# Moving the pools of the large tiles to the front of SBUF, behind a 384-byte pad, in a decode forward-and-backward kernel

## Chip, cores and metric

One core of one Trainium2 chip. The metric is the device time of one execution in microseconds (us), lower is better. A ratio is the mean time of one kernel's fast runs over the mean of the other's fast runs of the same rounds, so it is not quite the ratio of the medians that are quoted beside it. A difference under 2% is called "same"; the intervals are 95% intervals.

## The reference

Two attention layers on a long key and value cache and two small MLPs, for a batch of 2 and one token each, and then all gradients. Cut to what matters:

```python
B, Sq, D = 2, 1, 1024
Hq, Hkv, Sk, Dh = 32, 4, 16384, 128        # k_cache, v_cache: (2, 4, 16384, 128) bf16
# wq (1024, 4096), wo (4096, 1024); w1 (1024, 3584), w2 (3584, 1024)
x = x + attention(layernorm(x), k_cache, v_cache, wq, wo)
x = x + mlp(layernorm(x), w1, b1, w2, b2)
x = x + attention(layernorm(x), ...)       # the same weights and cache again
x = x + mlp(layernorm(x), ...)
# returned: x, and the gradients of x, k_cache, v_cache, wq, wo, w1, b1, w2, b2
```

The arithmetic per byte is tiny. The caches (33.6 MB each) are read several times, their gradients are written once.

## The kernel before

Transfers are nearly all of 1 MB: 128 partitions, 4096 bf16 values (8192 bytes) in each. Loads go out on the sync engine's queue, stores on GpSimd's. Seven rotating load tiles and ten kept tiles take all of them.

```python
LDW, NLD = 4096, 7
const = ctx.enter_context(tc.tile_pool(name="const", bufs=1))   # identities, masks
vec = ctx.enter_context(tc.tile_pool(name="vec", bufs=1))       # small vectors
pers = ctx.enter_context(tc.tile_pool(name="pers", bufs=1))     # e_all, 32768 bytes a partition
ld = ctx.enter_context(tc.tile_pool(name="ld", bufs=NLD))       # 7 load tiles of 8192 bytes
res = ctx.enter_context(tc.tile_pool(name="res", bufs=1))       # 10 kept tiles of 8192 bytes
ktp = ctx.enter_context(tc.tile_pool(name="ktp", bufs=4))       # and further pools
# ... cut ...
def w_load(W, j0, rb, n_cols):               # a chunk of a weight: rb rows of n_cols in a partition
    wt = ld.tile([128, LDW], BF16, name="wt", tag="ld")
    wv = wt[:, 0:rb * n_cols].rearrange("p (j n) -> p j n", j=rb)
    nc.sync.dma_start(wv, W[j0 * 128:(j0 + rb) * 128, :].rearrange("(j p) n -> p j n", p=128))
    return wv
# ... cut ...
def kv_load(w, g, c):                        # a chunk of a cache: one row of 8192 bytes in a partition
    keep = w + str(c) if g == G - 1 else w if (g, c) == (XG, 0) else None
    t = held_tiles[keep] if keep else ld.tile([128, LDW], BF16, name="kv_" + w, tag="ld")
    if keep not in held:
        src = Kv if w == "K" else Vv
        nc.sync.dma_start(t[:].rearrange("p (t d) -> p t d", d=128), src[g, :, c * TC:(c + 1) * TC, :])
        # ... cut ...
def store(out_ap, view, tile_):
    nc.gpsimd.dma_start(out_ap, view)
    by_store.append(tile_)                   # the tile is free for the next load
```

Until about 700 us there are nearly only loads (forward passes, and the backward parts that end in small vectors). From about 750 us on, the gradients of the caches and weights are made and stored while the caches are loaded once more, and load tiles and kept tiles serve both.

Tiles are laid out in the order of the pools, in steps of 32 bytes (the addresses here were read from the built programs, not from a trace). In the kernel before, the constants start at byte 16512 of the partition and e_all at 26048, which is 50 x 512 + 448. What follows it has sizes that are multiples of 512, so e_all, the seven load tiles and the ten kept tiles all begin 448 bytes past a multiple of 512, that is 192 past a multiple of 256.

## Time and profile before

| | before |
|---|---|
| median of 3 runs | 1155.29 us (1153.3 to 1155.74) |
| span of the profiled run, mean granted TensorE clock | 1151.1 us, 0.845 |
| moved by DMA | 449.30 MB, mean 390 GB/s |
| PE, DVE, ACT busy | 83%, 55%, 49% |

The page of the kernel before, the slices (40 of 28.8 us each; the first line has the busy share of the 16 DMA engines in tenths, the second what they moved) and the queues (q1 carries the loads, q0 the stores):

```profile
DMA  8999999998999999999999999888999999999996
GB/s 368 418 418 418 419 418 399 396 371 329 418 418 413 419 352 373 399 372 396 376 417 409 364 365 351 330 320 316 411 422 422 417 418 420 421 416 418 424 420 241
...
q1 hardware_dynamic: 72204, 348.17, 75.9%
q0 software_dynamic: 16752, 98.59, 20.7%
```

The engines for DMA are hardly ever idle, and there is a plateau of 418 GB/s in the slices with loads alone, and one of 418 to 424 in the last third, with stores beside the loads. The table by stretches says the same of chosen times. Its columns: from and to, length, then busy us and number of instructions of PE, weight loads, DVE, ACT and POOL, the granted clock, the DMA share and GB/s. The rows are two forward stretches (8192-byte rows), one with mostly rows of 2048 bytes (200 to 225 us), and two with stores.

```profile
50.00:150.00 100.00, 85.58 (x1625) 70.06 (x1622) 45.62 (x99) 42.45 (x190) 0.00 (x0) 0.85 1.01 418
300.00:400.00 100.00, 86.70 (x1709) 70.95 (x1701) 47.86 (x106) 44.53 (x201) 0.00 (x0) 0.90 1.01 417
200.00:225.00 25.00, 11.46 (x304) 10.44 (x304) 3.19 (x17) 0.00 (x0) 1.38 (x2) 0.50 1.01 396
...
850.00:950.00 100.00, 89.33 (x1146) 54.38 (x1146) 78.66 (x138) 72.12 (x139) 14.74 (x25) 0.80 1.01 420
1000.00:1100.00 100.00, 85.23 (x1165) 51.88 (x1165) 75.16 (x133) 70.31 (x136) 14.71 (x24) 0.85 1.02 420
```

A DMA share of 1.01 means that the packets' own times fill the stretch: there is no gap to close, and with the same bytes in the same rows only shorter packets can make it faster. The trace records every packet with its size and duration; a packet here is one row in one partition.

### The profile page before, as it was taken

What the parts mean: (1) busy time and instruction counts of PE and PEld (TensorE: products, weight loads), DVE (VectorE), ACT (ScalarE), POOL (GpSimd) and SP (SyncE); (2) the same over time, 40 slices, a digit from 0 to 9 for tenths busy, and PEclk for the clock granted to TensorE, in tenths of its full rate; (3) what the DMA queues carried; (4) which work ended last, traced back from release to release, by engine and by line L of the source; (5) the groups of instructions that cost most, each with busy time, mean ns of one, the idle gap of its engine ahead of it and who ended that gap; (6) DMA issues with size and microseconds to landing.
All of it is one profiled execution on the core that took longest, in us unless ns stands there. A gap on an engine that the chain in (4) does not pass through costs nothing. (4 is left out here: it accounts for less than half of the span.)

```text
span 1151.1 us, 39972 instructions
## 1 busy us (share of the span) xinstructions
PE 952.2 (83%) x17567; PEld 735.8 (64%) x17567; DVE 633.9 (55%) x1347; ACT 566.5 (49%) x1418; POOL 64.5 (6%) x117
## 2 busy tenths in 40 slices
PE   4989886487889875899998699988898998998786
PEld 3867674487767755898876588865555554555452
DVE  1545442132544441554746454678788866787684
ACT  0544351021544440344544344767677757687573
POOL 0000000000000000000000000001111111111111
PEclk9988886587997886899998899998888867799795
DMA  8999999998999999999999999888999999999996
GB/s 368 418 418 418 419 418 399 396 371 329 418 418 413 419 352 373 399 372 396 376 417 409 364 365 351 330 320 316 411 422 422 417 418 420 421 416 418 424 420 241
DMA packets 89130, 449.30 MB, mean 390 GB/s; under 512 B 7026, under 2 KB 7026, under 8 KB 49788
## 3 DMA queue, kind: packets, MB, share of 16 engines
q1 hardware_dynamic: 72204, 348.17, 75.9%
q0 software_dynamic: 16752, 98.59, 20.7%
q8 instruction: 137, 2.24, 0.8%
q14 instruction: 37, 0.30, 0.1%
HBM read 348.14 MB, written 98.58 MB: 388 GB/s over the span
## 5 line engine op out<-in xcount | busy, mean ns | idle before, releaser
L153 ACT COPY kT<-tp 128x512 int32<-128x512 int32 x209 | 122.6, 587 | 258.9 <-PE tp L419 248.2
L156 DVE COPY kT<-tp 128x1024 bf16<-128x1024 bf16 x159 | 108.7, 690 | 111.7 <-PE tp L419 99.8
L419 PE MATMUL tp<-ident,kv_K 128*128 128x128 bf16 x1728 | 145.6, 234 | 3.3 <-DMA kv_K<-in_A_k_cache_dram 3.3
L419 PEld LDWEIGHTS <-kv_K 128*128 128x128 bf16 x1728 | 110.7, 104 | 3.9 <-DMA kv_K<-in_A_k_cache_dram 3.8
L164 DVE CAST big<-xm 128x512 bf16<-128x512 f32 x135 | 88.1, 685 | 26.4 <-PE xm L1160 13.5
L161 ACT CAST big<-xm 128x512 bf16<-128x512 f32 x162 | 88.2, 593 | 27.0 <-PE xm L1160 15.7
L572 PEld LDWEIGHTS <-kT 128*128 128x128 bf16 x2048 | 76.8, 98 | 28.0 <-issue 22.2
L572 PE MATMUL sc<-qT_bf,kT 128*128 128x8 bf16 x2048 | 92.2, 171 | 0.5 <-issue 0.4
L269 PE MATMUL wtp<-ident,wt 128*128 128x128 bf16 x928 | 77.1, 231 | 3.8 <-issue 2.5
L419 PE MATMUL tp<-ident,kv_V 128*128 128x128 bf16 x864 | 71.0, 230 | 9.8 <-DMA kv_V<-in_A_v_cache_dram 9.0
L305 PEld LDWEIGHTS <-wt 128*128 128x128 bf16 x1696 | 48.9, 103 | 47.0 <-issue 15.4
L536 ACT ACTIVATE e_all<-sc,negm 128x64 bf16<-128x64 f32 x256 | 76.9, 344 | 1.1 <-DVE negm L531 1.0
L164 DVE CAST keepK<-xm 128x512 bf16<-128x512 f32 x91 | 59.0, 685 | 22.4 <-PE xm L1242 17.7
L451 PE MATMUL acc_all<-kv_V,e_all 128*16 128x256 bf16 x864 | 46.4, 294 | 29.0 <-DMA kv_V<-in_A_v_cache_dram 16.1
L156 DVE COPY wT<-wtp 128x1024 bf16<-128x1024 bf16 (+1 forms) x64 | 40.7, 641 | 50.8 <-PE wtp L269 47.3
L161 ACT CAST keepK<-xm 128x512 bf16<-128x512 f32 x105 | 56.8, 592 | 24.2 <-PE xm L1242 21.8
L153 ACT COPY wT<-wtp 128x512 int32<-128x512 int32 (+1 forms) x60 | 34.2, 571 | 66.2 <-PE wtp L269 57.5
L419 PEld LDWEIGHTS <-kv_V 128*128 128x128 bf16 x864 | 56.1, 103 | 11.7 <-DMA kv_V<-in_A_v_cache_dram 9.8
L269 PEld LDWEIGHTS <-wt 128*128 128x128 bf16 x928 | 58.8, 103 | 4.5 <-issue 3.1
L161 ACT CAST keepV<-xm 128x512 bf16<-128x512 f32 (+1 forms) x93 | 50.3, 594 | 21.6 <-PE xm L1242 16.8
L536 ACT ACTIVATION_READ_ACCUMULATOR e_all<-sc,negm 128x1 f32 x256 | 60.2, 236 | 0.0
L164 DVE CAST keepV<-xm 128x512 bf16<-128x512 f32 (+1 forms) x80 | 52.4, 685 | 12.7 <-PE xm L1242 9.1
(350 smaller groups left out, 1774.1 us busy)
## 6 DMA issues: line engine op xcount, KB each, us to landing
kv_K<-in_A_k_cache_dram SPq DMA_DIRECT2D x81, 1024.0 KB, 12.7
kv_V<-in_A_v_cache_dram SPq DMA_DIRECT2D x81, 1024.0 KB, 12.2
out_dram<-big POOLq DMA_DIRECT2D x36, 1024.0 KB, 21.0
wt<-in_A_wo_dram SPq DMA_DIRECT2D x32, 1024.0 KB, 10.6
wt<-in_B_w_dram SPq DMA_DIRECT2D x32, 896.0 KB, 14.6
out_dram<-keepK POOLq DMA_DIRECT2D x21, 1024.0 KB, 20.0
out_dram<-keepV POOLq DMA_DIRECT2D x19, 1024.0 KB, 18.6
wt<-in_A_wq_dram SPq DMA_DIRECT2D x16, 1024.0 KB, 9.2
```

The source lines that it names most:

```text
L153: S.copy(out=dst.bitcast(I32), in_=src.bitcast(I32))
L156: V.tensor_copy(out=dst, in_=src)
L161: S.copy(out=dst, in_=src)
L164: V.tensor_copy(out=dst, in_=src)
L269: PE.transpose(tp[:, o, :], wv[:, j, (o0 + o) * 128:(o0 + o + 1) * 128], ident[:])
L305: PE.matmul(fps[:, jo, :].rearrange("p (a b) -> p a b", b=2), lhsT=wv[:, j, jo * 128:(jo + 1) * 128], rhs=xT_bf[:, j0 + j, :].unsqueeze(1) ...
L419: PE.transpose(tp[:, j, :], cv[:, b * 8 + j, :], ident[:])
L451: PE.matmul(self.acc[cg:cg + 16, :], lhsT=coef(u), rhs=self.cv[:, t:t + 2, :].rearrange("p t d -> p (t d)"), start=False, stop=True, tile_ ...
L536: S.activation(out=e_all[:, g, f * half:(f + 1) * half, l, h, :], in_=sc[g][f][:, h, :].rearrange("p (a b) -> p a b", b=2), func=ACT.Exp, ...
L572: PE.matmul(sc[g][f][:, :, t % TH], lhsT=kT[:, j, :], rhs=q_bf[:, g, :], start=True, stop=True)
```

## The change

The intent: loads write into SBUF at starts that are a multiple of 512 bytes. The pools of the large tiles come first, behind a pad that fills up to the next multiple (16512 + 384 = 16896 = 33 x 512), and the pools with odd sizes come behind them. Nothing else is changed; both kernels have 39972 instructions and 89130 packets.

```diff
-    const = ctx.enter_context(tc.tile_pool(name="const", bufs=1))
-    vec = ctx.enter_context(tc.tile_pool(name="vec", bufs=1))
+    base = ctx.enter_context(tc.tile_pool(name="base", bufs=1))
+    base.tile([128, 192], BF16, name="to512")
     pers = ctx.enter_context(tc.tile_pool(name="pers", bufs=1))
     ld = ctx.enter_context(tc.tile_pool(name="ld", bufs=NLD))
     res = ctx.enter_context(tc.tile_pool(name="res", bufs=1))
+    const = ctx.enter_context(tc.tile_pool(name="const", bufs=1))
+    vec = ctx.enter_context(tc.tile_pool(name="vec", bufs=1))
     ktp = ctx.enter_context(tc.tile_pool(name="ktp", bufs=4))
```

## The prediction

> **What bounds the kernel now.** The page's slices show the DMA engines at 9 tenths or more almost everywhere, at 410 to 424 GB/s. The table by stretches gives a DMA share of 1.01 at 417 to 418 GB/s at 50 to 150 us (forward, loads alone), 1.02 at 420 GB/s at 825 to 1100 us (loads and stores), and 0.97 at 372 GB/s at 560 to 750 us, where PE and waits between engines count too. The queues add up to about 97% of 16 engines' span. So a change of a packet's time goes nearly in full into the kernel's time.
>
> **What the change does.** No instruction, transfer or wait is added or removed; only addresses move. In the layout of the kernel before, e_all, the seven load tiles and the ten kept tiles begin 448 bytes past a multiple of 512 (192 past a multiple of 256, on a multiple of 64). Afterwards they begin on 512. The small constants and vectors go behind them. Engine instructions should keep their durations (transposes about 230 ns, evacuations 587 to 690 ns in the groups).
>
> **What alignment can be worth.** The Trainium skill, "DMA: Bandwidth & Descriptors", section "How a descriptor splits into AXI transactions", says a descriptor off a 256-byte boundary starts with a transaction from the boundary below, and the unused bytes cost beats of 32 bytes: here 6. Estimate with that page's 32 B x 850 MHz per engine: 7 ns a packet, about 82,000 data packets over 16 engines, 36 us or 3%.
>
> The packet records do not look like that. Undisturbed times are 309 ns for 8192 bytes, 272 for 7168, 159 for 4096, 84 for 2048: bytes at 27.2 GB/s plus a constant 8 to 9 ns. The same constant appears where the large tiles play no part or alignment varies: 4-byte completion packets take 9 ns; the instruction queue's 8192-byte packets start at 307 to 309 ns; the sixteen 128-byte stores of a bias row all take 13 ns and the sixteen 448-byte stores 25 ns, although their starts fall at different offsets within 256 bytes. So I read it as per-packet cost, not misalignment.
>
> What is left is the excess over that floor: in pure load stretches 8192-byte packets have a median of 312 ns and a mean near 315; beside stores 309 to 311, with the same misaligned tiles. If all of it were alignment, about 5 ns on 31,000 packets over 16 engines is 10 us; I give it a fifth, 2 us.
>
> **On the critical path.** Practically all of those 2 us, since the load stretches are DMA-bound. Removed 2, added 0.
>
> **Prediction.** 1153 us, 8 in 10 between 1143 and 1160. Faster by over 2%: 0.05; within 2%: 0.93; slower: 0.02.
>
> **What would show it.** Right: the same bytes and packet counts, 416 to 420 GB/s at 50 to 150 us, the queues' shares within half a point, matmul and copy groups within 1%. Wrong in "constant is per-packet": the forward slices rise to 425 or more, the weight stretch of 2048-byte packets (200 to 250 us, now 396 GB/s) gains most, up to 8%, and the load queue's share falls by two points. Wrong in "engines don't care": weight loads, matmul or copy groups shift by several per cent.
>
> **What would make it wrong.** The profile may report a write into SBUF as it is accepted, not as it ends, hiding a partial first write; the sixteen-store evidence is for reading SBUF only. Moved constants might cost engines time that no record of before shows. A shift of the granted clock (0.845 mean) could hide the effect.

## More of the kernel before

Landmarks for later, the instructions of two lines of the kernel before (when the output of the first and second attention is ready, and that of the first and second MLP):

```profile
L761 DVE TENSOR_TENSOR xA<-acc_all,xT x1: 175/175/175, 210.7 to 210.7; 128x16 f32<-128x16 f32 x1
L761 DVE TENSOR_TENSOR xA<-acc_all,xM x1: 175/175/175, 439.1 to 439.1; 128x16 f32<-128x16 f32 x1
...
L793 DVE TENSOR_TENSOR xM<-xM,xA x2: 176/176/176, 262.6 to 696.6; 128x16 f32<-128x16 f32 x2
```

## The result

1143.36 us median of 4 runs (1142.54 to 1144.22) against 1155.4 us (1153.3 to 1155.74): 12 us less, ratio 0.990 (0.9882 to 0.9917). That is within 2% and at the lower edge of the range, and six times the 2 us that the prediction gave. The mean granted clock of the profiled runs hardly differs (0.845 before, 0.847 after).

The page of the kernel after, slices and queues (slices of 28.5 us):

```profile
DMA  9999999998999989999999999887999999999996
GB/s 371 424 424 424 425 423 413 408 379 354 423 424 424 425 302 424 410 377 407 373 423 419 349 354 355 314 331 309 400 423 422 421 420 422 423 422 421 424 419 247
...
q1 hardware_dynamic: 72204, 348.17, 75.4%
q0 software_dynamic: 16752, 98.59, 20.8%
```

The table by stretches of the kernel after, same columns and times:

```profile
50.00:150.00 100.00, 86.35 (x1662) 70.31 (x1658) 46.45 (x101) 44.47 (x203) 0.00 (x0) 0.86 1.01 424
300.00:400.00 100.00, 87.36 (x1739) 70.93 (x1739) 47.75 (x109) 46.07 (x202) 0.00 (x0) 0.91 1.01 424
200.00:225.00 25.00, 11.90 (x327) 10.99 (x328) 3.19 (x17) 0.00 (x0) 1.39 (x2) 0.50 1.01 408
...
850.00:950.00 100.00, 89.07 (x1162) 54.92 (x1159) 78.83 (x139) 73.72 (x142) 15.32 (x26) 0.83 1.02 421
1000.00:1100.00 100.00, 90.25 (x1230) 56.22 (x1228) 76.76 (x135) 71.01 (x137) 14.25 (x24) 0.81 1.02 422
```

The stretches with loads alone rose from 417 or 418 to 424 GB/s, and the one with 2048-byte rows from 396 to 408. Beside stores the rate is nearly what it was. In both kernels the DMA share is 1.01 or 1.02: the engines are just as full, but with shorter packets. The same landmarks in the kernel after (its line numbers are two higher):

```profile
L763 DVE TENSOR_TENSOR xA<-acc_all,xT x1: 174/174/174, 206.8 to 206.8; 128x16 f32<-128x16 f32 x1
L763 DVE TENSOR_TENSOR xA<-acc_all,xM x1: 175/175/175, 430.8 to 430.8; 128x16 f32<-128x16 f32 x1
...
L795 DVE TENSOR_TENSOR xM<-xM,xA x2: 174/175/176, 256.4 to 685.8; 128x16 f32<-128x16 f32 x2
```

Subtract line by line: 3.9 us gained at the first attention's end, 6.2 at the first MLP's, 8.3 at the second attention's, 10.8 at the second MLP's. The spans differ by 10.3. So in this pair of traces all of the gain is there by 697 us, and the last 440 us, in which the stores lie, add none. (Each trace is a single run; the traces of all full kernels are compared under e6 and e7.)

The packet records, worked out from the trace (median / mean, ns):

| packets | before | after |
|---|---|---|
| loads of 8192 bytes, 50 to 150 us | 312 / 315.5 | 309 / 310.7 |
| loads of 2048 bytes, 195 to 215 us | 88 / 88.7 | 84 / 84.3 |
| loads of 8192 bytes beside stores, 850 to 1100 us | 309 / 311.6 | 309 / 310.8 |
| stores of 8192 bytes, 850 to 1100 us | 309 / 312.4 | 309 / 310.9 |

Before 439 us the kernel before has 17152 loads of 8192 bytes, 11781 of 2048 and about 1130 of 7168. At the 4.4 to 4.8 ns of these windows for each and 16 engines that would make (30,100 x 4.4 to 4.8)/16 = 8.3 to 9.0 us. Summed over all records up to the landmark, slow packets included, it is a little less: the load queue's packets fell from 427.1 to 419.4 us of 16 engines' time (7.7 us), those of all queues from 431.2 to 423.0 (8.2 us), because the mean of the 2048-byte rows fell by only 3.0 ns there. The landmark moved by 8.3.

### The profile page after: what moved, and what is told of

Read it like the earlier page. It is cut to its first block, busy times and chain, and to the rows that moved or that the text cites. A ratio compares the mean times of both kernels' runs of the same rounds, so it can differ in the third digit from the quotient of the medians.

```text
span 1140.8 us, 39972 instructions
## 1 busy us (share of the span) xinstructions
PE 954.6 (84%) x17567; PEld 736.6 (65%) x17567; DVE 633.4 (56%) x1347; ACT 566.2 (50%) x1418; POOL 64.7 (6%) x117
## 2 busy tenths in 40 slices
DMA packets 89130, 449.30 MB, mean 394 GB/s; under 512 B 7026, under 2 KB 7026, under 8 KB 49788
## 5 line engine op out<-in xcount | busy, mean ns | idle before, releaser
L271 PE MATMUL wtp<-ident,wt 128*128 128x128 bf16 x928 | 73.9, 225 | 3.7 <-issue 2.5
```

The costliest lines, as they stand in the source:

```text
L271: PE.transpose(tp[:, o, :], wv[:, j, (o0 + o) * 128:(o0 + o + 1) * 128], ident[:])
```

## The experiments

Nine kernels ran. All seven full kernels gave correct results. The kernel before was timed beside each group, at medians of 1155.18, 1156.43 and 1154.15 us.

The theory: a load that writes into SBUF from a start off a boundary has longer packets, by some nanoseconds each, and in stretches of loads alone that goes straight into the time. Rivals: the new order of the pools, or e_all's place, helps the engines; the boundary is 512, as the change says; the cost grows with the offset; the stretches with stores gain as well.

### e1_order_448: the new order without the alignment

```diff
-    base.tile([128, 192], BF16, name="to512")
+    base.tile([128, 160], BF16, name="to448")
```

> The order of the changed kernel, with a pad of 320 instead of 384 bytes, so that every large tile starts 448 bytes past a multiple of 512 again. Theory (writes of loads into off-boundary tiles are slower): time back to 1155 us, ratio to before 0.998 to 1.003, 8192-byte load packets in the pure load stretches back to a median of 312 ns, 417 to 418 GB/s at 50 to 150 us. Rival (the new order, with constants and vectors behind the large tiles, helps the engines): stays at 1143 us, ratio 0.99.

Measured: 1156.17 us, ratio 0.9996 (0.9964 to 1.0027); 418 GB/s at 50 to 150 us; load packets there 312 / 315.4 ns. From the table by stretches:

```profile
50.00:150.00 100.00, 85.29 (x1621) 69.30 (x1622) 44.21 (x96) 42.38 (x191) 0.00 (x0) 0.85 1.01 418
```

The whole gain is gone although the order is the new one. The order is not the cause.

### e2_pad_only: the alignment without the new order

On the kernel before:

```diff
+    base = ctx.enter_context(tc.tile_pool(name="base", bufs=1))
+    base.tile([128, 32], BF16, name="to512")
     pers = ctx.enter_context(tc.tile_pool(name="pers", bufs=1))
```

> The order of the kernel before, with a pad of 64 bytes ahead of e_all, so that the large tiles start on multiples of 512 without any reordering. Theory (alignment of the load tiles alone): 1143 us, ratio 0.988 to 0.992, load packets at a median of 309 ns, 424 GB/s at 50 to 150 us. Rival (order): 1155 us, ratio 1.0.

Measured: 1143.64 us, ratio 0.9893 (0.9868 to 0.9918); 424 GB/s; load packets 309 / 310.6 ns.

```profile
50.00:150.00 100.00, 83.82 (x1632) 68.31 (x1625) 45.34 (x100) 43.05 (x194) 0.00 (x0) 0.88 1.01 424
```

A pad of 64 bytes gives all of the gain.

### e4_eall_only: e_all on 512, the load and kept tiles not

```diff
     pers = ctx.enter_context(tc.tile_pool(name="pers", bufs=1))
+    off = ctx.enter_context(tc.tile_pool(name="off", bufs=1))
+    off.tile([128, 224], BF16, name="off448")
     ld = ctx.enter_context(tc.tile_pool(name="ld", bufs=NLD))
```

> The changed kernel with a second pad of 448 bytes between e_all and the load tiles: e_all starts on 512, load and kept tiles 448 bytes past it. Theory (only what loads write into matters): 1155 us, ratio 0.998 to 1.003. Rival (e_all's place helps the engines that read it in every score and accumulation): most of the gain stays, ratio about 0.99.

Measured: 1158.51 us, ratio 1.0017 (0.9987 to 1.0048); 418 GB/s. Putting e_all, which only the engines read and write, on the boundary gains nothing by itself.

### b1_sweep: loads alone at nine starts

A kernel that only moves data. It computes nothing, so its result is wrong. Seven tiles with room for an offset; each stretch has 28 loads of 1 MB and a wait for all of them at its end.

```diff
+    def view(i, off):
+        return tiles[i % 7][:, off // 2:off // 2 + 4096]
+    for off in (0, 448, 192, 64, 32, 128, 256, 320, 384, 0, 448):
+        for i in range(28):
+            nc.sync.dma_start(view(i, off)..., Kv[g, :, t, :])
+        end()          # small copies that read all seven tiles
```

> A measurement, with a wrong result on purpose: stretches of 28 loads of 1 MB in 8192-byte rows into seven tiles, at starts of 0, 448, 192, 64, 32, 128, 256, 320, 384, 0 and 448 bytes past 512; then loads of 2048-byte rows at 448 and 0; then stores at 448 and 0; then loads beside stores at 448 and 0. Theory (a load into SBUF pays for starting off a boundary): 424 GB/s at 0 and 417 to 418 at 448; whichever other starts are fast name the boundary (256 fast means 256 is enough; 64 fast means 64 is enough, which the case of 448 speaks against). The 2048-byte rows gain more, 84 against 88 ns; stores and the mixed stretch show no difference over 0.5%. Rival (the alignment has no effect on the transfers): every stretch of loads within 0.3%.

The middle of each stretch in the table by stretches of this kernel. Its columns are busy us of DVE and POOL, the clock, the DMA share and GB/s; the rows are the starts 0, 448, 192, 64, 32, 128, 256, 320, 384, 0 and 448 in this order.

```profile
14.00:62.00 48.00, 2.39 (x3) 0.00 (x0) 1.00 1.01 427
87.00:135.00 48.00, 0.00 (x0) 0.00 (x0) 1.00 1.01 423
160.00:208.00 48.00, 0.00 (x0) 0.00 (x0) 1.00 1.01 422
233.00:281.00 48.00, 0.00 (x0) 0.00 (x0) 1.00 1.01 422
305.00:353.00 48.00, 0.00 (x0) 0.00 (x0) 1.00 1.01 421
379.00:427.00 48.00, 0.00 (x0) 0.00 (x0) 1.00 1.01 423
451.00:499.00 48.00, 0.00 (x0) 0.00 (x0) 1.00 1.01 428
523.00:571.00 48.00, 0.00 (x0) 0.00 (x0) 1.00 1.01 423
597.00:645.00 48.00, 0.00 (x0) 0.00 (x0) 1.00 1.01 422
669.00:717.00 48.00, 0.00 (x0) 0.00 (x0) 1.00 1.01 428
741.00:789.00 48.00, 0.00 (x0) 0.00 (x0) 1.00 1.01 423
```

Two levels and nothing between: 427 or 428 at 0 and 256, 421 to 423 everywhere else. In the packet records the middle 80% of a stretch have a mean of 309.0 ns at 256 and at the second 0, and 312.9 to 314.1 at the seven starts off the boundary; 32 bytes off costs as much as 192. (The first stretch, also at 0, has the median of 309 too, but about 30 slow packets lift its mean to 312.7.) This has no engine at work beside the DMA, so it is not a collision with one. The rates were all a little higher than expected (424 and 417 to 418); the difference is as expected. The kernel's later stretches ran into one another: of the 2048-byte pair, the first (448) had a median of 88 ns and the second (0) 84, with some stores already beside it, and the stores could not be told apart. They were measured again in b2_sides.

### e3_off256: is 256 enough?

```diff
-    base.tile([128, 192], BF16, name="to512")
+    base.tile([128, 64], BF16, name="to256")
```

> The changed kernel with a pad of 128 bytes: large tiles start on 256 but not on 512. Theory (a load write pays for crossing 256-byte boundaries, as the sweep's fast stretch at 256 said): 1143 us, ratio 0.988 to 0.992, 424 GB/s at 50 to 150 us. Rival (512 bytes is the boundary, as the change's name has it): 1155 us, ratio 1.0.

Measured: 1143.78 us, ratio 0.9893 (0.9872 to 0.9913); 424 GB/s; 309 / 310.7 ns. The boundary is 256 bytes, not 512.

### e5_off32: is a small offset cheaper?

```diff
-    base.tile([128, 192], BF16, name="to512")
+    base.tile([128, 208], BF16, name="to32")
```

> The changed kernel with large tiles 32 bytes past a multiple of 512. Theory (one more transaction a packet, a cost that doesn't grow with the offset, 4 ns at every start off 256): 1155 us, ratio 0.997 to 1.003, 417 to 418 GB/s at 50 to 150 us. Rival (the cost is the bytes below the start, in beats of 32: one beat here, six at 448): a sixth of the loss, 1145 us, ratio about 0.992.

Measured: 1156.35 us, ratio 1.0000 (0.9979 to 1.0022); 417 GB/s; 313 / 316.3 ns. A start 32 bytes past the boundary loses everything. The cost does not grow with the offset.

### b2_sides: row lengths, stores, and the HBM side

Another kernel that only moves data, with starts of 448 and 0 for each case. Its output is wrong, which doesn't matter for the time. The source of the shorter rows is column slices of wq; the offset in HBM is put on a flat view of the cache or of its gradient.

```diff
+    def hbm(f, i, off):
+        a = i % 31 * 524288 + off // 2
+        return f[a:a + 524288].rearrange("(p x) -> p x", p=128)
+    # loads: 8192-, 4096-, 2048-, 1024-byte rows at 448, 0; source off by 448
+    # stores at 448, 0; destination off by 448; loads beside stores at 448, 0; 8192 again
```

> A measurement, with a wrong result on purpose: 28 transfers of 1 MB a stretch, apart from each other. Loads in rows of 8192, 4096, 2048 and 1024 bytes, each into SBUF starts of 448 and then 0; loads whose source in HBM is 448 bytes off and whose tile is on 512; stores from SBUF starts of 448 and 0; stores to HBM 448 bytes off from tiles on 512; loads beside stores at 448 and 0; loads of 8192 at 448 and 0 again. Theory (one more write transaction a packet): loads at 448 cost the same 4 ns more a packet at every row length, so 1.3% at 8192 and about 5% at 2048 bytes; stores from 448 and the mixed stretch show under 0.5% between 448 and 0. Rival (a cost per byte): the same share at every row length. Open, with no forecast: the two stretches that are off in HBM.

Loads, the middle of each stretch in this kernel's table by stretches, same columns as for b1_sweep; pairs of 448 and 0 for rows of 8192, 4096, 2048 and 1024 bytes, and at the end 8192 once more:

```profile
14.00:64.00 50.00, 2.39 (x3) 0.00 (x0) 1.00 1.01 422
88.00:138.00 50.00, 0.00 (x0) 0.00 (x0) 1.00 1.01 427
160.00:215.00 55.00, 0.00 (x0) 0.00 (x0) 1.00 1.03 410
237.00:287.00 50.00, 0.00 (x0) 0.00 (x0) 1.00 1.03 421
312.00:366.00 54.00, 0.00 (x0) 0.00 (x0) 1.00 1.05 387
392.00:442.00 50.00, 0.00 (x0) 0.00 (x0) 1.00 1.05 409
467.00:530.00 63.00, 0.00 (x0) 0.00 (x0) 1.00 1.09 348
555.00:610.00 55.00, 0.00 (x0) 0.00 (x0) 1.00 1.09 386
...
1206.00:1254.00 48.00, 0.00 (x0) 0.00 (x0) 1.00 1.01 423
1278.00:1328.00 50.00, 0.00 (x0) 0.00 (x0) 1.00 1.01 427
```

The packets of the middle 80% of those stretches:

| row bytes | mean ns at 448 | at 0 | difference | loss of rate |
|---|---|---|---|---|
| 8192 (last pair) | 313.0 | 309.1 | 3.9 | 1% |
| 4096 | 163.4 | 159.0 | 4.4 | 3% |
| 2048 | 88.7 | 84.0 | 4.7 | 5% |
| 1024 | 51.2 | 46.0 | 5.2 | 10% |

So it is a cost per packet, 4 to 5 ns, nearly the same at an eighth of the length. A cost per byte would have shrunk to an eighth.

Stores and mixtures, in the same view: stores from 448, from 0, stores to a place in HBM 448 bytes off, then loads beside stores at 448 and at 0.

```profile
700.00:755.00 55.00, 1.07 (x21) 14.22 (x27) 1.00 1.01 422
770.00:825.00 55.00, 0.00 (x0) 9.77 (x19) 1.00 1.01 422
845.00:900.00 55.00, 0.00 (x0) 11.15 (x21) 1.00 1.01 412
940.00:1030.00 90.00, 0.00 (x0) 9.03 (x17) 1.00 1.01 425
1080.00:1170.00 90.00, 0.00 (x0) 8.50 (x16) 1.00 1.01 428
```

Stores do not care where in SBUF they read (422 and 422 GB/s). Beside stores, the loads' packets take 309.0 ns at both starts: they no longer show the cost. The mixed stretches still differ by 0.7%, over the 0.5% expected; the stores in the first of them have a few slow packets (mean 313.3 ns, 90th percentile 309, 99th 548) and in the second none. The pair at the end of b1_sweep, 448 and then 0, shows the same:

```profile
1120.00:1210.00 90.00, 0.00 (x0) 9.30 (x18) 1.00 1.01 423
1265.00:1355.00 90.00, 0.00 (x0) 9.86 (x19) 1.00 1.01 428
```

There too the loads' packets take 309.0 to 309.1 ns at both starts, and only the stores at 448 have slow packets (mean 315.9 ns, 99th percentile 580). But in both kernels the slow packets lie in the first half of the stretch at 448 (420 and 421 GB/s, then 428), and 448 came first both times, directly after stores alone. So start and order are not told apart, and the cause stays open. A store whose destination in HBM is off lost 2.4% (412 against 422), a load whose source is off under 1% (packets 310.6 against 309.1 ns, with some stores beside it), in one stretch each. In these stretches the two offsets that cost over 1% are those of the side that is written. Nothing in the kernel studied does either.

### e6_ld_only and e7_res_only: which tiles, and which stage

The load tiles alone on 512, and the kept tiles alone on 512, both on the kernel after:

```diff
 e6_ld_only
     ld = ctx.enter_context(tc.tile_pool(name="ld", bufs=NLD))
+    off = ctx.enter_context(tc.tile_pool(name="off", bufs=1))
+    off.tile([128, 224], BF16, name="off_pad")
     res = ctx.enter_context(tc.tile_pool(name="res", bufs=1))
 e7_res_only
+    off = ctx.enter_context(tc.tile_pool(name="off", bufs=1))
+    off.tile([128, 224], BF16, name="off_pad")
     ld = ctx.enter_context(tc.tile_pool(name="ld", bufs=NLD))
+    back = ctx.enter_context(tc.tile_pool(name="back", bufs=1))
+    back.tile([128, 32], BF16, name="back_pad")
     res = ctx.enter_context(tc.tile_pool(name="res", bufs=1))
```

> The changed kernel with the seven load tiles (and e_all) on 512 and the ten kept tiles 448 bytes past it. Until about 700 us nearly all loads go into the seven load tiles (ten of the first loads go into kept tiles); after 750 us loads and stores share all seventeen. Theory (the gain is that of loads without stores beside them): nearly all of it stays, 1143 to 1145 us, ratio 0.988 to 0.993. Rival (the last 400 us gain too, by the tiles' share): 1147 to 1150 us, ratio 0.993 to 0.996.

Measured: 1143.43 us, ratio 0.9906 (0.9881 to 0.9931).

> The other way round: the ten kept tiles (and e_all) on 512, the seven load tiles 448 bytes past it. Theory: nothing left of the gain, 1154 to 1156 us, ratio 0.997 to 1.003. Rival: a third of the gain, 1150 to 1152 us, ratio 0.995 to 0.997.

Measured: 1154.26 us, ratio 1.0001 (0.9979 to 1.0023).

The seven load tiles give all of the gain, the ten kept tiles none that can be seen, although they are more than half of the tiles that loads and stores share after 750 us. That agrees with the landmarks: nearly all of the gain is that of loads with no stores beside them.

How far "nearly" goes, the traces of all nine full kernels say, one run each. In the four with the load tiles on a multiple of 256, the second MLP's landmark starts at 685.8 to 688.6 us, in the other five at 695.9 to 699.4: 10.1 us between the means. The spans differ by 12.4 us. What follows the landmark takes 453.1 to 455.0 us in the four and 454.4 to 458.0 in the five, so up to about 2 us of the gain may lie there, and the scatter hides whether they do. The stores' packets between 850 and 1100 us have a mean of 310.9 to 311.2 ns in the four and 311.9 to 313.0 in the five; why is not shown.

## Why the prediction was right or wrong

- **Right: the DMA engines bound the kernel, and a packet's time goes into the kernel's time.** The records of all packets up to the landmark at 439 us sum to 8.2 us less, and the landmark moved 8.3 us.
- **Right: the 8 to 9 ns over the bytes' time is a per-packet constant and not misalignment.** The undisturbed times of 309, 272, 159 and 84 ns are the same after the change.
- **Right: engines don't care.** Transposes of K took 234 ns before and 233 after, the largest copies 587 and 690 ns before, 587 and 691 after. Two groups moved by more than the 1% forecast, transposes of weights from 231 to 225 ns and those of V from 230 to 227. They did not make the time: in e2_pad_only, with the whole gain, they took 233 and 231 ns.
- **Wrong in size: "If all of it were alignment, about 5 ns on 31,000 packets over 16 engines is 10 us; I give it a fifth, 2 us."** The step that failed is that fifth. In loads alone alignment was all of the excess in the median (312 to 309 ns) and about three quarters in the mean, which fell from 315.5 to 310.7 ns, 4.8 of the 6.5 above the floor of 309. The sum also left out the 2048-byte rows, 31,749 load packets: their excess over 84 ns fell from 4.7 to 0.3 ns at 195 to 215 us. The term of 2 us measured 10 to 12 us. That 1143.36 us still lies in the range of 1143 to 1160, by 0.36 us, is luck: nothing in the sum pointed there.
- **The clue that was misread:** the same tiles showed 309 to 311 ns beside stores, and that was taken as a sign that the excess was not alignment. But a load's packet does not show this cost when about as many stores run beside it, as b2_sides shows (309.0 ns at both starts).
- **The reservation that came true:** the evidence of the sixteen-packet stores was for reading SBUF only. Stores pay nothing (422 and 422 GB/s), loads do, and the prediction carried the one over to the other.
- **Of the signs that were named,** 416 to 420 GB/s at 50 to 150 us failed (424), which is just short of the "425 or more" that was to tell against the constant: between the two lay the case that happened. The 2048-byte stretch did gain most, as named against the constant, but 3% (396 to 408 GB/s) where up to 8% was said. The queues' shares stayed within half a point as said, but this was a poor test, since the span shrank with them: summed over the records, the load queue's packets took 873.5 us of 16 engines' time before and 860.6 after, 12.9 us less.

Shown are the boundary, the cost per packet, and that loads without stores pay it. That the extra time is one more write for the piece of a row on the far side of the boundary fits those, but no record shows the write itself, so this is inferred. Why a load's packet does not show the cost beside stores is open too.

## What to carry to other kernels

Where a stretch is bound by loads and the DMA share is full, check the start of the load tiles in their partition, and fill up to a multiple of 256 bytes: here a 64-byte pad did as much as reordering all pools. Expect 4 to 5 ns a packet, so about 1% at rows of 8192 bytes, 5% at 2048 and 10% at 1024. Beside stores this case shows no such gain: the loads' packets are as short either way, and what is left there is at most about 2 us of 440. When a packet's median is a few ns over its undisturbed time in one stage and not in another, treat it as something to explain, and work out its sum over all row lengths before calling it small.

## What the Trainium skill lacked or had wrong

- "DMA: Bandwidth & Descriptors", section "How a descriptor splits into AXI transactions": its 256-byte boundary agrees with these runs (starts at 0 and 256: 427 or 428 GB/s, all others 421 to 423). Its account by beats, in which the bytes below the start are paid for, doesn't fit loads into SBUF: 32 bytes off (one beat) cost 5.1 ns a packet and 192 off (six beats) 4.4 ns. It is worded for reads (the bytes below the start are "fetched but unused"), but stores that read SBUF 448 bytes off lost nothing (422 and 422 GB/s), and the loads above pay for where they write.
- The same page has no figure for a load beside stores: the loads' packets did not show the cost there (309.0 ns at both starts), and the full kernel gained at most about 2 us after 697 us. Nor for the HBM side: stores to HBM 448 bytes off ran at 412 against 422 GB/s.
- "SBUF — State Buffer", section "Operand start alignment", says of its own that it is about legality and that its runs timed nothing. What a load without stores beside it pays: 4 to 5 ns a packet off a multiple of 256 bytes, 1% of this kernel's time.
